# Set attention and a gated feed-forward on one core: the weight words converted with VectorE masks, fewer GpSimd operations, a new instruction order

## The chip, the cores and the metric

The kernel runs on one core of a Trainium2 chip. The metric is device time in microseconds (us) of one execution; what is given as "the time" is the median of three executions. A profiled execution leaves a trace. Its span runs from the first to the last recorded instruction or transfer, and the time of that execution is a little longer than the span. Engines are named as the profile names them: PE is TensorE's matmul, PEld its weight load, DVE is VectorE, ACT is ScalarE, POOL is GpSimd, SP (SPq) is SyncE's DMA queue.

## What is computed

```python
def _attn_ref(x, inducing):             # x 4 x 12480 x 128, inducing 32 x 128
    def mab(q, kv):
        s = scale * (q @ kv.transpose(0, 2, 1))
        a = np.exp(s - s.max(-1, keepdims=True))
        a /= a.sum(-1, keepdims=True) + 1e-09
        return a @ kv
    h = mab(I, x)                        # 32 inducing rows attend to all tokens of a batch
    return mab(x, h)                     # every token attends to those 32 rows
def _moe_ref(x, w_in, w_out):            # w_in 128 x 2048, w_out 2048 x 128
    h = x @ w_in
    return (h - np.tanh(h)) @ w_out
```

x is float32. w_in and w_out come as float64, which the core reads as pairs of 32-bit words.

## The kernel before, in words

Each of the four batches (12480 tokens) is cut into seven slabs of 1792 tokens, 896 KB each (`big` tiles, 19 of them, shared by all uses). A batch has a first and a second half.

**First half** (`first`): all seven slabs are loaded (line 397) and scored on PE against the inducing rows (`scores`, line 382 with `indT_sb`). Two slabs share a PSUM tile `d`, which DVE copies to an `sl` tile while it takes the maximum (line 409). The maximum over the whole batch (lines 422 to 427) must be known before ACT can take the first exponential (line 436). DVE transposes those (line 438, tile `et`, two of them), and PE accumulates them against the slab in token order (`acc`, line 473). The slab in token order is either loaded a second time (13 slabs, `LOADED`, line 448) or made by PE transposes (line 458) and copied out of PSUM by ACT (line 464) or DVE (line 466).

**Linear part** (`linear`): the 32 attended rows (`hT`, lines 486 to 494) go through the feed-forward. Instead of h - tanh(h) for every token, the kernel uses a tangent at the mean of the 32 rows of a batch: products with w_in (line 382, `win_sb`), a transpose and the mean on DVE (lines 516 to 521), tanh on ACT, an odd series in the mean (`series`, lines 529 to 533, five small DVE operations), the tangent (lines 538 to 542), and products with w_out (line 551 and lines 557, 558), which end in the small tiles P4 and Pm (lines 560, 561).

**Second half** (`second`): every slab is scored against `hT` (line 382), copied out with a maximum (line 595); per group of slab pairs the maximum is spread (lines 602 to 608), ACT takes exponentials (line 619), PE multiplies with P4 (line 634), and ACT (line 650) or DVE (line 652) writes the result to a `big` tile, which is stored (line 641). A batch's first half runs beside the second half of the batch before. A bound for the tangent (`bound`) is computed at the end; a general path behind it isn't taken.

**Weights** (`weight`): eight chunks of 128x512 double words, four of w_in, four of w_out. Each is loaded to a `big` tile as raw words, and low word, exponent, mantissa and sign are taken apart and put together on DVE, ACT and GpSimd. A chunk's `big` tile comes free, and can take the next slab, when the chunk is done.

**What sets the order.** `Plan.order` simulates five in-order queues (PE, DVE, ACT, POOL, SP) with a cost for each operation, and picks among the ready operations by priority. The priorities come from constants (`LOADX`, `PA`, `OT` and others) and from `JIT`, a table of offsets by kind, batch and slab. The instructions are then issued in that order, and each engine works its own list strictly in order: an instruction that waits holds up all behind it. SP's list holds every load and store.

## Time and profile before

| | us |
|---|---|
| median of 3 runs (191.67 to 192.47) | 191.79 |
| the profiled execution | 191.85 |
| its span | 190.1 |
| PE busy | 151.0 |
| DVE busy | 137.8 |
| ACT busy | 104.7 |
| POOL busy | 46.5 |
| 67.39 MB in SP's DMA queue, share of 16 engines | 89.5% |

The kernel has a head (weights and the first half of batch 0, to about 50 us), a middle in which the halves of neighbouring batches run beside each other, and a tail in which batch 3 is finished and stored. Shares of busy time are means over these three, so each is read by itself.

### The profile page before, as it was taken

The page shows a single profiled execution, that of the slowest core. Times are in us where ns is not written, and L with a number is a line of the kernel's source. Part 1 is how long each engine was busy: PE and PEld are TensorE (multiplying, and loading weights), DVE is VectorE, ACT ScalarE, POOL GpSimd, SP SyncE. Part 2 cuts the span into 40 slices and gives each one's busy share as a digit, 9 for nine tenths or more (in the row PEclk, how much of TensorE's full clock was granted, in tenths as well). Part 3 has the DMA queues.
Part 4 walks back from the last instruction along what each step waited for, and adds up shares of the span by engine and source line. Part 5 has one row for each costly group of instructions (what it writes and reads, how often), then busy time and mean ns, then how long its engine had stood idle before and what let it go on. Part 6 is the DMA issues. An engine that isn't in the chain of part 4 may idle for free.

```text
span 190.1 us, 4686 instructions
## 1 busy us (share of the span) xinstructions
PE 151.0 (79%) x1924; PEld 85.9 (45%) x1924; DVE 137.8 (73%) x292; ACT 104.7 (55%) x156; POOL 46.5 (24%) x38
## 2 busy tenths in 40 slices
PE   0059987517999999999989999989999997896600
PEld 0006746207855647664267663545466323352100
DVE  3438978655739989676998378986975899898900
ACT  2716857891013294465196734456957467679900
POOL 1499999599902000000200000200000020000000
PEclk9999996855999999999999999999999999999955
DMA  5999999605999999999999999998999997589993
GB/s 119 406 392 428 416 409 422 228 0 186 365 397 418 401 393 399 406 400 364 396 416 409 422 402 411 394 428 322 326 420 424 413 376 297 205 331 401 375 400 145
DMA packets 11549, 67.77 MB, mean 357 GB/s; under 512 B 1408, under 2 KB 1408, under 8 KB 11520
## 3 DMA queue, kind: packets, MB, share of 16 engines
q1 hardware_dynamic: 11520, 67.39, 89.5%
q8 instruction: 17, 0.28, 0.5%
q14 instruction: 12, 0.10, 0.1%
HBM read 41.83 MB, written 25.56 MB: 355 GB/s over the span
## 4 chain that ended last, share of the span: by engine, by line
PE 45%; DMA 20%; POOL 9%; ACT 7%; DVE 6%; issue 6%; SPq 1%; DVEq 0%; POOLq 0%; ACTq 0%
PE d L382 14%; DMA big<-in_xT 12%; PE side L473 8%; PE d L634 8%; PE d L458 8%; DMA big<-in_xn 6%; POOL big L348 5%; ACT big L650 3%; DMA big<-in_w_in 2%; PE side L551 2%; DVE big L652 2%; POOL win_sb L359 2%; POOL win_sb L362 1%; PE side L605 1%; PE side L382 1%
## 5 line engine op out<-in xcount | busy, mean ns | idle before, releaser
L650 ACT ACTIVATE big<-d,Pm,wg 128x896 f32<-128x896 f32 x31 | 33.6, 1094 | 29.0 <-PE d L634 24.7
L382 PE MATMUL d<-big,indT_sb 128*32 128x448 f32 x224 | 29.2, 590 | 12.7 <-DMA big<-in_xT 12.4
L473 PE MATMUL side<-big,et 128*32 128x128 f32 x784 | 30.4, 287 | 5.6 <-DVE et L438 4.9
L458 PE MATMUL d<-ident,big 128*128 128x128 f32 x210 | 29.6, 295 | 3.6 <-DVE big L466 2.2
L464 ACT COPY big<-d 128x896 f32<-128x896 f32 x23 | 20.3, 905 | 22.0 <-PE d L458 21.7
L473 PEld LDWEIGHTS side<-big,et 128*32 128x32 f32 x784 | 25.0, 115 | 16.4 <-DVE et L438 7.8
L634 PE MATMUL d<-sl,k 32*128 32x448 f32 x212 | 30.4, 585 | 0.2
L458 PEld LDWEIGHTS d<-ident,big 128*128 128x128 f32 x210 | 25.2, 152 | 11.8 <-DVE big L466 3.0
L652 DVE TENSOR_SCALAR big<-d,wg,Pm 128x896 f32<-128x896 f32 x22 | 26.6, 1208 | 4.4 <-PE d L634 3.3
L382 PE MATMUL d<-big,hT 128*32 128x448 f32 x224 | 25.3, 542 | 1.0 <-ACT big L650 0.6
L564 POOL TENSOR_TENSOR m<-m,all_mean 128x512 f32<-128x512 f32 x4 | 4.2, 1048 | 60.9 <-DVE all_mean L521 60.9
L438 DVE STREAM_TRANSPOSE et<-sl 128x896 f32<-128x896 f32 (+1 forms) x16 | 15.7, 983 | 2.8 <-issue 2.8
L409 DVE TENSOR_SCALAR_CACHE_REDUCE sl<-d 128x896 f32<-128x896 f32 (+1 forms) x16 | 15.3, 967 | 3.2 <-PE d L382 2.3
L595 DVE TENSOR_SCALAR_CACHE_REDUCE sl<-d 128x896 f32<-128x896 f32 (+1 forms) x16 | 15.3, 964 | 3.0 <-PE d L382 3.0
L348 POOL TENSOR_SCALAR big<-big 128x512 int32<-128x512 f32 x8 | 15.7, 1968 | 6.4 <-ACT big L344 5.9
L619 ACT ACTIVATE sl<-sl,nbs 128x896 f32<-128x896 f32 (+1 forms) x16 | 14.9, 945 | 3.0 <-DVE nbs L608 3.0
L634 PEld LDWEIGHTS d<-sl,k 32*128 32x128 f32 x212 | 9.9, 183 | 13.2 <-issue 4.9
L382 PEld LDWEIGHTS d<-big,indT_sb 128*32 128x32 f32 x224 | 6.3, 112 | 20.8 <-issue 12.6
L436 ACT ACTIVATE sl<-sl,nb 128x896 f32<-128x896 f32 (+1 forms) x16 | 15.1, 945 | 0.2 <-DVE nb L427 0.2
L352 DVE SCALAR_TENSOR_TENSOR big<-big 128x512 uint32<-128x512 uint32 x8 | 5.5, 693 | 9.9 <-POOL big L348 9.9
L382 PEld LDWEIGHTS d<-big,hT 128*32 128x32 f32 x224 | 7.1, 109 | 9.2 <-issue 7.2
L414 POOL MEMSET sl<- 64x32 f32 x4 | 0.7, 174 | 39.7 <-DVE sl L409 39.7
(112 smaller groups left out, 169.3 us busy)
## 6 DMA issues: line engine op xcount, KB each, us to landing
big<-in_xT SPq DMA_DIRECT2D x28, 896.0 KB, 9.0
outT<-big SPq DMA_DIRECT2D x23, 896.0 KB, 6.3
big<-in_xn SPq DMA_DIRECT2D x13, 896.0 KB, 9.8
outT<-big SPq DMA_DIRECT2D x3, 864.0 KB, 8.4
big<-in_w_in SPq DMA_DIRECT2D x4, 512.0 KB, 6.9
big<-in_w_out SPq DMA_DIRECT2D x4, 512.0 KB, 14.7
outT<-big SPq DMA_DIRECT2D x3, 448.0 KB, 6.1
outT<-big SPq DMA_DIRECT2D x1, 416.0 KB, 6.9
```

The source lines that it names most:

```text
L348: nc.gpsimd.tensor_scalar(out=x.bitcast(I32), in0=x.bitcast(F32), scalar1=255.0, scalar2=8388608.0, op0=ALU.min, op1=ALU.mult)
L382: nc.tensor.matmul(ps[q * m:(q + 1) * m, :n], lhsT=w, rhs=row, start=True, stop=True)
L409: nc.vector.tensor_scalar(out=sl.get()[:, :n, :], in0=ps.get()[:, :n, :W], scalar1=1.0, scalar2=None, op0=ALU.mult, op1=ALU.max, accum_out ...
L436: nc.scalar.activation(out=t, in_=t, func=AF.Exp, scale=SC, bias=nb.get(), accum_out=sums.get()[:, g:g + 1])
L438: add("DVE", 0.16 + 0.00103 * W * len(pair), lambda e, et=et, sl=sl, n=len(pair): nc.vector.transpose(out=et.get()[:, :n * KB, :].rearrang ...
L458: nc.tensor.transpose(out=o[:, k * 128:(k + 1) * 128], in_=x.get()[:, at:at + 128], identity=ident)
L464: nc.scalar.copy(out=dst, in_=src)
L473: nc.tensor.matmul(hacc.get()[q * m:(q + 1) * m, :C], lhsT=et.get()[:, j * KB + k, :], rhs=xn_t.get()[:, k * C:(k + 1) * C], start=at < NQ ...
L595: nc.vector.tensor_scalar(out=sl.get()[:, :n, :], in0=ps.get()[:, :n, :W], scalar1=1.0, scalar2=None, op0=ALU.mult, op1=ALU.max, accum_out ...
L634: nc.tensor.matmul(ds[q // 2].get()[:, q % 2, :W], lhsT=P4.get()[r, :], rhs=sl.get()[r, j, :], start=True, stop=True)
L650: nc.scalar.activation(out=dst, in_=src, func=AF.Identity, scale=wg.get(), bias=Pm.get())
L652: nc.vector.tensor_scalar(out=dst, in0=src, scalar1=wg.get(), scalar2=Pm.get(), op0=ALU.mult, op1=ALU.add)
```

## The change

Four things change. The weights' bits are taken apart in another way: the exponent is only masked on DVE, the mantissa gets the exponent of 8.0 by a second mask, ACT makes the power's bits directly in one operation that existed before with another scale (`above`), ACT's `mantissa` and GpSimd's `power` are gone, and `join` moves from GpSimd to DVE, where it subtracts the 7 as well. GpSimd keeps one operation per chunk (`scale`). The series moves from DVE to GpSimd and has six operations there. The planner's costs and constants change, and so do all offsets in `JIT`, `SIDE`, `LOADED` (13 slabs as before, partly others) and the groups: batch 1 is grouped as three pairs and one, and batch 3 as two and two, where it was four single pairs (eight groups instead of ten).

```diff
 JIT = {
-    ('A', 0, 0): -2, ('A', 0, 1): 7, ('A', 0, 2): -8, ('A', 0, 3): -17, ('A', 0, 4): 2, ('A', 0, 5): -32,
...
+    ('A', 0, 0): -110, ('A', 0, 1): 10, ('A', 0, 2): -10, ('A', 0, 3): 3, ('A', 0, 4): -10, ('A', 0, 5): -128,
...
-LATE = -5.0
-WAIT = 0.30000000000000004
-LOADW = (-32.5, -27.0)
-PA, OT, PT, OB, PB = 4.5, 17.5, 8.5, -5.0, 16.5
-LOADX, LOADN = 32, 154.5
-SWITCH = 11.5
+LATE = 10.0
+WAIT = -11.700000000000006
+LOADW = (-31.5, -27.0)
+PA, OT, PT, OB, PB = -8.0, 25.0, 11.0, -17.5, 16.0
+LOADX, LOADN = 32, 313.5
+SPLITS = ([[0, 1], [2, 3]], [[0], [1], [2], [3]], [[0, 1], [2], [3]], [[0, 1, 2, 3]], [[0, 1, 2], [3]], [[0], [1, 2, 3]])
+SPLIT = (0, 4, 0, 0)
+SWITCH = 12.5
...
-    GROUPS = [[[0, 1], [2, 3]]] * (B - 1) + [[[0], [1], [2], [3]]]
+    GROUPS = [SPLITS[k] for k in SPLIT]
...
-        v.memset(shift[:, 0:1], -896.0)
+        v.memset(shift[:, 0:1], -896.0 * 2.0 ** 23)
...
+            def exponent(e, r=r):
+                nc.vector.tensor_scalar(out=r["e"], in0=r["hi"], scalar1=0x7FF00000, scalar2=None, op0=ALU.bitwise_and)
+
+            def bits(e, r=r, dst=dst):
+                nc.vector.tensor_scalar(out=dst.bitcast(U32), in0=r["hi"], scalar1=0xFFFFF, scalar2=0x41000000,
+                                        op0=ALU.bitwise_and, op1=ALU.bitwise_or)
+
             def low(e, r=r):
                 nc.scalar.activation(out=r["lo"].bitcast(F32), in_=r["lo"], func=AF.Copy, scale=2.0 ** -52)
 
-            def exponent(e, r=r):
-                nc.vector.tensor_scalar(out=r["e"], in0=r["hi"], scalar1=20, scalar2=0x7FF,
-                                        op0=ALU.logical_shift_right, op1=ALU.bitwise_and)
-
-            def bits(e, r=r, dst=dst):
-                nc.vector.tensor_scalar(out=dst.bitcast(U32), in0=r["hi"], scalar1=0xFFFFF, scalar2=None, op0=ALU.bitwise_and)
-
             def above(e, r=r):
-                nc.scalar.activation(out=r["e"].bitcast(F32), in_=r["e"], func=AF.Relu, bias=shift[:, 0:1])
-
-            def power(e, r=r):
-                x = r["e"]
-                nc.gpsimd.tensor_scalar(out=x.bitcast(I32), in0=x.bitcast(F32), scalar1=255.0, scalar2=8388608.0, op0=ALU.min, op1=ALU.mult)
+                nc.scalar.activation(out=r["e"], in_=r["e"], func=AF.Relu, scale=8.0, bias=shift[:, 0:1])
...
-            def mantissa(e, dst=dst):
-                nc.scalar.activation(out=dst, in_=dst.bitcast(U32), func=AF.Copy, scale=2.0 ** -20, bias=1.0)
-
             def join(e, r=r, dst=dst):
-                nc.gpsimd.tensor_tensor(out=dst, in0=dst, in1=r["lo"].bitcast(F32), op=ALU.add)
+                nc.vector.scalar_tensor_tensor(out=dst, in0=dst, scalar=-7.0, in1=r["lo"].bitcast(F32), op0=ALU.add, op1=ALU.add)
...
         def series(e):
-            v = nc.vector
+            v = nc.gpsimd
             a, q, y = u.get(), g.get(), mean.get()
             v.tensor_tensor(out=a, in0=y, in1=y, op=ALU.mult)
             v.tensor_scalar(out=q, in0=a, scalar1=SERIES[2], scalar2=SERIES[1], op0=ALU.mult, op1=ALU.add)
             v.tensor_tensor(out=q, in0=q, in1=a, op=ALU.mult)
-            v.scalar_tensor_tensor(out=q, in0=q, scalar=SERIES[0], in1=a, op0=ALU.add, op1=ALU.mult)
+            v.tensor_scalar(out=q, in0=q, scalar1=SERIES[0], scalar2=None, op0=ALU.add)
+            v.tensor_tensor(out=q, in0=q, in1=a, op=ALU.mult)
             v.tensor_tensor(out=q, in0=q, in1=y, op=ALU.mult)
```

In the changed kernel the lines have other numbers: exponent 339, bits 342, sign 353, join 357, scale 360, the copy with maximum 405, exponentials 432, transposes 434, accumulation 469, series 525 to 530, tangent 535 to 539, second-half copies 592, results 647 (ACT) and 649 (DVE).

What moves is shown at two places. The first is GpSimd's list in the head, where `big` and `win_sb` are the chunks' tiles. Before:

```order
L348 TENSOR_SCALAR big_65<-big_65 128x512
L359 TENSOR_TENSOR win_sb<-win_sb,big_65 128x512
L348 TENSOR_SCALAR big_66<-big_66 128x512
L362 TENSOR_TENSOR win_sb<-win_sb,big_65 128x512
L359 TENSOR_TENSOR win_sb<-win_sb,big_66 128x512
L348 TENSOR_SCALAR big_68<-big_68 128x512
```

Now:

```order
L360 TENSOR_TENSOR win_sb<-win_sb,big_66 128x512
L360 TENSOR_TENSOR win_sb<-win_sb,big_67 128x512
L360 TENSOR_TENSOR win_sb<-win_sb,big_69 128x512
L360 TENSOR_TENSOR win_sb<-win_sb,big_71 128x512
L360 TENSOR_TENSOR wout_sb<-wout_sb,big_76 128x512
```

Two of GpSimd's three operations for each chunk are gone from its list. On DVE, at the same place in the head, the list was:

```order
L352 SCALAR_TENSOR_TENSOR big_65<-big_65 128x512
L352 SCALAR_TENSOR_TENSOR big_66<-big_66 128x512
L337 TENSOR_SCALAR big_68<-big_68 128x512
L341 TENSOR_SCALAR win_sb<-big_68 128x512
L409 TENSOR_SCALAR sl_84,mxg_196<-d_95 128x896
L352 SCALAR_TENSOR_TENSOR big_68<-big_68 128x512
L337 TENSOR_SCALAR big_71<-big_71 128x512
L341 TENSOR_SCALAR win_sb<-big_71 128x512
```

and is now:

```order
L357 SCALAR_TENSOR_TENSOR win_sb<-win_sb,big_66 128x512
L353 SCALAR_TENSOR_TENSOR big_66<-big_66 128x512
L339 TENSOR_SCALAR big_67<-big_67 128x512
L342 TENSOR_SCALAR win_sb<-big_67 128x512
L357 SCALAR_TENSOR_TENSOR win_sb<-win_sb,big_67 128x512
L405 TENSOR_SCALAR sl_84,mxg_185<-d_95 128x896
L353 SCALAR_TENSOR_TENSOR big_67<-big_67 128x512
L339 TENSOR_SCALAR big_69<-big_69 128x512
L342 TENSOR_SCALAR win_sb<-big_69 128x512
```

Each chunk has a fourth DVE operation, the join, and the two masks of the next chunk (339 and 342) stand right behind the operation that releases GpSimd's only one.

The second place is DVE in the tail, from the mean of batch 3 (`all_mean`) to the tangent (`m_99` is the slope tile that PE waits for). Before:

```order
L521 TENSOR_SCALAR all_mean<-all_mean 128x16
L595 TENSOR_SCALAR sl_89,bm_1567<-d_96 128x896
L652 TENSOR_SCALAR big_81<-d_95,wg_1557,Pm_1316 128x896
L529 TENSOR_TENSOR u_1582<-all_mean 128x16
L530 TENSOR_SCALAR all_g<-u_1582 128x16
L531 TENSOR_TENSOR all_g<-all_g,u_1582 128x16
L532 SCALAR_TENSOR_TENSOR all_g<-all_g,u_1582 128x16
L533 TENSOR_TENSOR all_g<-all_g,all_mean 128x16
L602 TENSOR_REDUCE big_1593<-bm_1567 128x1
L603 TENSOR_SCALAR k_101<-ident,big_1593 128x128
L538 TENSOR_TENSOR all_gp<-th_1569 128x16
L539 TENSOR_TENSOR m_99<-m_98,all_gp 128x512
```

Now:

```order
L517 TENSOR_SCALAR all_mean<-all_mean 128x16
L592 TENSOR_SCALAR sl_84,bm_1547<-d_97 128x896
L649 TENSOR_SCALAR big_82<-d_96,wg_1539,Pm_1478 128x896
L535 TENSOR_TENSOR all_gp<-th_1572 128x16
L536 TENSOR_TENSOR m_99<-m_98,all_gp 128x512
```

The five series operations and the two of a group's maximum no longer stand between the mean and the tangent. PE's list behind it, from the products with w_out to the points (`mean_w`), was:

```order
L551 MATMUL side<-wout_sb,m_99 32x128 x16
L382 MATMUL d_97<-big_75,hT_119 32x448 x4
L382 MATMUL d_97<-big_65,hT_119 32x448 x4
L634 MATMUL d_95<-sl_91,k_103 128x448 x2
L634 MATMUL d_96<-sl_91,k_103 128x448 x2
L557 MATMUL side<-k_105,fold 128x128
L558 MATMUL side<-mean_w,k_105 128x1
```

and is now:

```order
L631 MATMUL d_96<-sl_89,k_104 128x448 x2
L548 MATMUL side<-wout_sb,m_99 32x128 x16
L378 MATMUL d_95<-big_69,hT_119 32x448 x4
L554 MATMUL side<-k_103,fold 128x128
L555 MATMUL side<-mean_w,k_103 128x1
```

One scored slab stands between the two products, where there were two scored slabs and one multiplied with P4.

## Rows read from the trace of the kernel before

**Rows 1.** Page, slices of the span in 40 equal parts: POOL, DMA share, GB/s.

```profile
POOL 1499999599902000000200000200000020000000
...
DMA  5999999605999999999999999998999997589993
GB/s 119 406 392 428 416 409 422 228 0 186 365 397 418 401 393 399 406 400 364 396 416 409 422 402 411 394 428 322 326 420 424 413 376 297 205 331 401 375 400 145
```

**Rows 2.** Windows: stretch, its length, busy us (count) by engine, clock, DMA, GB/s.

```profile
38.00:40.00 2.00, 0.95 (x8) 0.00 (x0) 1.82 (x2) 2.00 (x4) 1.92 (x2) 0.50 0.00 0
...
60.00:80.00 20.00, 20.00 (x319) 12.17 (x315) 16.79 (x40) 10.03 (x20) 0.97 (x2) 1.00 1.00 401
```

**Rows 3.** Chain that ended last, in order of time: start, us, what.

```profile
48.47 11.10 DMA big<-in_xT
...
75.49 0.96 PE d L634 x8
76.45 1.00 PE side L473 x28
```

**Rows 4.** Instructions grouped by line and form: count | busy us, mean ns | idle before.

```profile
L438 DVE STREAM_TRANSPOSE et<-sl 128x896 f32<-128x896 f32 x12 | 13.1, 1101 | 2.8 <-issue 2.8
L409 DVE TENSOR_SCALAR_CACHE_REDUCE sl<-d 128x896 f32<-128x896 f32 x12 | 13.0, 1082 | 2.3 <-PE d L382 2.3
...
L466 DVE COPY big<-d 128x896 f32<-128x896 f32 x7 | 7.5, 1080 | 1.9 <-PE d L458 1.2 <-ACT big L464 0.8
...
L352 DVE SCALAR_TENSOR_TENSOR big<-big 128x512 uint32<-128x512 uint32 x8 | 5.5, 693 | 9.9 <-POOL big L348 9.9
...
L564 POOL TENSOR_TENSOR m<-m,all_mean 128x512 f32<-128x512 f32 x4 | 4.2, 1048 | 60.9 <-DVE all_mean L521 60.9
...
L356 ACT ACTIVATE wout_sb<-wout_sb 128x512 f32<-128x512 uint32 x4 | 2.5, 623 | 1.9 <-DVE wout_sb L341 1.9
...
L533 DVE TENSOR_TENSOR all_g<-all_g,all_mean 128x16 f32<-128x16 f32 x4 | 0.7, 175 | 0.1
...
L414 POOL MEMSET sl<- 64x32 f32 x4 | 0.7, 174 | 39.7 <-DVE sl L409 39.7
```

**Rows 5.** Single lines: durations in ns as minimum, median, maximum; first and last start.

```profile
L337 DVE TENSOR_SCALAR big<-big x8: 422/998/1522, 5.8 to 38.8; 128x512 uint32<-128x512 uint32 x8
...
L362 POOL TENSOR_TENSOR wout_sb<-wout_sb,big x4: 1272/1312/1772, 32.6 to 50.7; 128x512 f32<-128x512 f32 x4
```

**Rows 6.** Instructions in order of time, head: start us, us, engine, line, what.

```profile
9.39 1.72 PE L382 MATMUL d<-big,indT_sb 128*32 128x448 f32 x8 [9.39 <-DMA big<-in_xT]
...
25.29 0.69 DVE L352 SCALAR_TENSOR_TENSOR big<-big 128x512 uint32<-128x512 uint32 x1 [1.18 <-POOL big L348]
25.34 1.80 POOL L359 TENSOR_TENSOR win_sb<-win_sb,big 128x512 f32<-128x512 f32 x1
25.90 1.52 DVE L337 TENSOR_SCALAR big<-big 128x512 uint32<-128x512 uint32 x1
...
33.99 0.96 PE L382 MATMUL d<-big,indT_sb 128*32 128x448 f32 x8
...
35.11 0.62 DVE L409 TENSOR_SCALAR_CACHE_REDUCE sl<-d 128x448 f32<-128x448 f32 x1 [0.93 <-ACT big L464]
...
37.53 1.04 ACT L436 ACTIVATE sl<-sl,nb 128x896 f32<-128x896 f32 x1 [0.19 <-DVE nb L427]
...
42.72 1.10 DVE L438 STREAM_TRANSPOSE et<-sl 128x896 f32<-128x896 f32 x1
...
49.37 0.64 DVE L438 STREAM_TRANSPOSE et<-sl 128x448 f32<-128x448 f32 x1
```

**Rows 7.** SP's DMA queue in order of time: start us, us, line, what, count.

```profile
61.46 1.08 SPq L397 DMA_DIRECT2D big<-in_xT  x2
```

**Rows 8.** Instructions in order of time, tail (batch 3's linear part).

```profile
147.39 0.35 DVE L489 TENSOR_SCALAR k<-side,rs 128x128 f32<-128x128 f32 x1
...
164.08 0.26 ACT L560 COPY k<-side 128x128 f32<-128x128 f32 x1
```

More of the change, by code (lines that the diff above doesn't have):

```diff
@@ L296, in fused_kernel @@
     mean_b, gp_b, g_b, far_b = ([stacked(n, b) for b in range(B)] for n in ("mean", "gp", "g", "far"))
-    add("SP", 0.1, lambda e: nc.sync.dma_start(out=indT_sb, in_=indT), writes=[ind_b], pri=-500, size=0.02)
+    add("SP", 0.35, lambda e: nc.sync.dma_start(out=indT_sb, in_=indT), writes=[ind_b], pri=-500, size=0.02)
     add("POOL", 0.6, lambda e: make_identity(nc, ident), writes=[ident_b], pri=-10)
@@ L364, in weight @@
             p = pri + k
-            add("SP", 0.1, ld, writes=[buf], pri=load_pri + k, size=0.524)
-            add("DVE", 0.7, exponent, reads=[buf], writes=[ex], pri=p)
-            add("ACT", 0.7, low, reads=[buf], writes=[lo], pri=p)
-            add("ACT", 0.7, above, reads=[buf, ones_b], writes=[ex], pri=p)
-            add("DVE", 0.7, bits, reads=[buf], writes=[outs[k]], pri=p)
-            add("ACT", 0.7, mantissa, reads=[buf], writes=[outs[k]], pri=p)
-            add("POOL", 0.75, power, reads=[buf], writes=[ex], pri=p)
-            add("DVE", 0.8, sign, reads=[buf], writes=[ex], pri=p)
-            add("POOL", 1.4, join, reads=[buf, lo], writes=[outs[k]], pri=p)
-            add("POOL", 1.4, scale, reads=[buf, ex], writes=[outs[k]], pri=p)
+            add("SP", 0.35, ld, writes=[buf], pri=load_pri + k, size=0.524)
+            add("DVE", 0.55, exponent, reads=[buf], writes=[ex], pri=p)
+            add("DVE", 0.55, bits, reads=[buf], writes=[outs[k]], pri=p)
+            add("ACT", 0.68, low, reads=[buf], writes=[lo], pri=p)
+            add("ACT", 0.71, above, reads=[buf, ones_b], writes=[ex], pri=p)
+            add("DVE", 0.75, sign, reads=[buf], writes=[ex], pri=p)
+            add("DVE", 0.75, join, reads=[buf, lo], writes=[outs[k]], pri=p)
+            add("POOL", 1.45, scale, reads=[buf, ex], writes=[outs[k]], pri=p)
     xT_b = {}
@@ L396, in first @@
                 base = b * N + BASE[s]
-                add("SP", 0.1, lambda e, x=x, base=base: nc.sync.dma_start(out=x.get(), in_=xT[:, base:base + ST]),
+                add("SP", 0.35, lambda e, x=x, base=base: nc.sync.dma_start(out=x.get(), in_=xT[:, base:base + ST]),
                     writes=[x], pri=pri + s - LOADX + jit("X", b, s), size=0.9175)
@@ L423, in spread_out @@
             nc.vector.tensor_scalar(out=mq.get(), in0=mask, scalar1=mx.get(), scalar2=None, op0=ALU.mult)
-        add("DVE", 0.35, spread_out, reads=[mxg, fold_b], writes=[mq], pri=p)
+        add("DVE", 0.42, spread_out, reads=[mxg, fold_b], writes=[mq], pri=p)
         add("PE", 0.25, lambda e: nc.tensor.matmul(ps.get()[:, :NQ], lhsT=fold2, rhs=mq.get(), start=True, stop=True),
@@ L542, in tangent @@
             v.tensor_tensor(out=WM.get(), in0=WM.get(), in1=wide(k), op=ALU.add)
-        add("DVE", 0.6, series, reads=[mean], writes=[u, g], pri=pri)
-        add("DVE", 1.75, tangent, reads=[MT, th, g, mean], writes=[gp, WM, k], pri=pri)
+        add("POOL", 1.5, series, reads=[mean], writes=[u, g], pri=pri)
+        add("DVE", 1.92, tangent, reads=[MT, th, g, mean], writes=[gp, WM, k], pri=pri)
         psP, psR = place("q"), place("q")
@@ L640, in store @@
                     def store(at, end, needs):
-                        add("SP", 0.1, lambda e: nc.sync.dma_start(out=outT[:, base + at:base + end], in_=ot.get()[:, at:end]),
+                        add("SP", 0.35, lambda e: nc.sync.dma_start(out=outT[:, base + at:base + end], in_=ot.get()[:, at:end]),
                             reads=[ot, *needs], pri=pri - 200, size=0.9175 * (end - at) / ST)
```

12 lines of the change are left out of this document (6 added, 6 removed), and 51 rows, old and new, of the table JIT.

## The prediction, made before the changed kernel was run

> **What bounds the kernel now.** I read the slices of the page first [rows 1]. DMA is full from 3 to about 33 us and nearly full from 50 to 155 us, but between lies a hole: two slices of 4.75 us in which it moves 228 and 0 GB/s on average, and the one after moves 186. In just these slices GpSimd is at 9 tenths. It is the only long stretch in which GpSimd is busy, and it is the weights' conversion. The window from 38 to 40 us shows the hole from inside: no byte, PE busy half the time at a granted clock of 0.50 (1.2 GHz, the lower of its two levels), ACT and GpSimd full [rows 2]. The chain of waits tells what the hole costs: a transfer of a slab, 11.1 us long on the chain, that begins only at 48.47 us [rows 3]. The loads behind it wait for `big` tiles that the weight chunks hold.
>
> The second bound is PE. From 60 to 80 us PE is busy for 20.00 of 20 us [rows 2], and the chain runs through PE alone there, about 1 us for each slab and step [rows 3]. So the middle is paid for by PE's work, which the change leaves as it is, but for two spreads of a group's maximum. DMA has room behind that: 67.39 MB at the 400 to 420 GB/s of the full slices [rows 1] are 164 us. What the head wins is therefore kept by the middle, and what it doesn't win the middle can't give. The tail is a chain from the last accumulation of batch 3 to P4, then stores.
>
> **Weights: what goes, what comes.** Per chunk GpSimd had three operations (power, join, scale; about 2.0 + 1.7 + 1.5 us) and keeps the scale, 1.27 us alone and up to 1.77 us next to DVE [rows 5]. So GpSimd falls from some 41 us of conversion to 8 x 1.5 = 12 us and bounds nothing any more. ACT loses eight mantissa operations of 0.62 us [rows 4], 5 us in all, in a stage where it isn't the last to arrive: I count nothing for it. The operation that now makes the power's bits existed before, so it is free. DVE gets eight joins of the form of the sign operation, 0.69 us [rows 4]: 5.5 us. That makes DVE the engine to look at in the head.
>
> DVE's masks have two prices. Line 337 takes 0.42 us at best and 1.52 us at worst [rows 5], and the row of 25.90 us shows the bad case: the mask starts inside a GpSimd operation that runs from 25.34 to 27.14, and ends 0.28 us after it [rows 6]. The sign operation ahead of it started with that GpSimd operation and took its usual 0.69 us; GpSimd's took 1.80 instead. In the new order the two masks of the next chunk stand right behind the operation that starts GpSimd's scale, so one of each pair is held: 1.50 + 0.43 = 1.93 us a pair.
>
> The Trainium skill (SBUF — State Buffer, section SBUF: two separate sides) says that GpSimd and a DVE operation in a two-port mode, or one with two SBUF inputs, lock each other out for a whole instruction, whoever starts first. The masks' rows agree with it; that a join could be held too, which it also says, no row shows, since every sign operation came first.
>
> **The head, from both sides.** The point to watch is the first exponential, at 37.53 us before [rows 6]; it needs all seven slabs of batch 0 scored. *Earliest*: up to the seventh slab lie the same 9.57 MB in both orders (seven slabs of 0.9175 MB and six chunks of 0.524). 1.97 MB had landed when PE started at 9.39 us [rows 6]; the other 7.6 MB at 0.41 MB/us are 18.5 us, so it lands at 27.9. Scoring it started at 33.99 before, 3.5 us ahead of the exponential [rows 6]. So not before 31.4 us. *By DVE's list*: the first chunk now comes behind a slab, 1.44 MB; between 5.8 us (0.52 MB, [rows 5]) and 9.39 us (1.97 MB) that is 8.1 us. From there to the copy of the seventh slab (line 405) DVE has one free pair of masks 0.9, five held pairs 9.7, ten joins and signs 6.9, three copies of scores 3.2 and two copies of transposed slabs 2.2 (1.08 us each, [rows 4]): 22.9 us, so 31.0 us. From that copy to the exponential it was 37.53 - 35.11 = 2.4 us, and one join stands between: 34.1 us. I take 34.1, since DVE's sum lies above the data's and each of its terms is a row; waits between DVE, ACT and PE could add 2 us. Gain: 3.4 us (bounds 1.5 and 6).
>
> From there to the release of batch 2's first slab load, which came at 61.46 us [rows 7]. Before, the first transpose (42.72) waited some 4 us for DVE, which stood at a sign operation behind GpSimd's power, and the last one ended at 50.0 [rows 6]. Now DVE has, from 33.9 us on: a held pair 1.9, a free mask 0.4, a held mask 1.5, four joins and signs 2.8, transposes of 3 x 1.10 + 0.63 [rows 4, 6]: 10.6 us, so the last ends at 44.5. Behind it PE has two accumulations and two slabs' scores of about 1 us each [rows 3], the small steps to `hT` 1.5, one more scoring, seven transposes 0.9, the products with w_in 1.1 and the first scoring with `hT` 0.75: 8.3 us, plus about 1 us that it lags: 54.0. Gain: 7.5 us. The two gains are not added, the second contains the first.
>
> Can the loads follow? A slab takes 2.24 us at 0.41 MB/us. The queue in front of the load that needs the sixth chunk's tile runs dry at about 35 us; that chunk's scale ends at about 34.5. The load behind waits for the first accumulation, at about 37.5, so 1 to 2 us of hole remain where there were 10. DMA then ends the eighth load behind the hole at about 56, against 63 us (45 us, where it restarted, plus 8 x 2.24), so it keeps step.
>
> Not all is gain: PE's new list has at that point one scoring less behind it, and at the first product with P4 (75.49 us before, [rows 3]) one scoring and one accumulation less, 0.96 + 1.0 = 1.9 us that are still to do.
>
> **Series on GpSimd.** DVE loses five operations of about 0.18 us [rows 4] per batch. What six cost on GpSimd no row shows: between 0.17 us each (a memset of 32 elements) and 1.05 us (a product of 512 elements, [rows 4]), 1.0 to 6.3 us. I take 0.3 us each, 1.8 us, near the low end since 16 elements are nearer to 32 than to 512, with a start for each. Between the mean and the first DVE operation that needs the series, DVE's new list has two other operations (1.1 + 1.2 us) and three of the tangent (1.0 us): 3.3 us of cover, so I cost it at nothing; uncovered, at the high end, it is 3.0 us a batch.
>
> [...]
>
> **Order and groups.** ACT hands DVE four result copies and one copy of a transposed slab: in the middle DVE is at 16.8 of 20 us [rows 2] and the series' 3.5 us make up for part of the 5.9, so nothing. Two groups fewer save PE 0.8 us, hidden in rounding. In the tail, from the last accumulated product (147.39 + 0.35) to P4 (164.08 + 0.26) it was 16.6 us [rows 8]. The new lists drop from that path the series 0.9, a group's maximum 0.4, and on PE one scoring and one product (1.7); they add a result copy ahead of the mean (1.2), and the products with w_in come 1.1 us later behind two scorings but `hT` 1.1 us earlier. Sum -1.8; I take -2, bounds -4 and +1. Behind P4 eight slabs are stored in both, so the end follows P4.
>
> **Sum.** 190.1 - 7.5 + 1.9 - 2.0 = 182.5 us of span. The profiled execution took 191.85, that is 1.75 us more than its span and 0.06 from the median: 184.3 us.
>
> **Rivals.**
> 1. *The head goes at the data's pace.* If the masks mostly slip in ahead of GpSimd, the exponential comes at 31.4 us, 2.7 earlier: 181.5 us. For it: a mask at 0.42 us occurs in the trace. Against it: the median mask is at 1.0 [rows 5].
> 2. *The joins are held as well.* A join that starts inside a scale would wait out its rest, up to 1.3 us [rows 5]; with three or four of the six on the path the head loses 4 us of its 7.5: 188.3 us. For it: DVE's list is the longest in the head by my sum. Against it: there is one GpSimd operation for a chunk, and a mask mostly meets it first.
> 3. *The order gives it back in the middle.* DVE's copies come later in the new order's lists and PE waits for `d` tiles, of which there are three. PE is 20.00 of 20 [rows 2] before, so there is nothing to win there and something to lose: waits of a tenth over the 70 us of the middle are 7 us, 191.3 us, no change. Against it: I find no place for it in the lists.
> 4. *The series becomes the path (slower).* If a small GpSimd operation costs near the 1.05 us of line 564, DVE stops at the tangent with everything behind it (copies of scores, results), PE waits for the slope and for `d`: (6 x 1.05 - 3.3) x 4 = 12 us, 196 us. It decides from about 0.9 us an operation: then 4 x 2.1 = 8.4 us take away the gain of 7.6. Against it: line 564 works on 32 times the elements.
>
> **How the numbers follow.** Chances: forecast (183 to 187) 0.50, rival 1 0.17, rival 2 0.15, rival 3 0.10 (two thirds of it within the bound, one third slower), rival 4 0.08. Faster by over 0.5% (about what a measurement here can tell from no change) is below 190.8: 0.50 + 0.17 + 0.15 = 0.82; same 0.07; slower 0.11. The range leaves out rivals 3 and 4: up to 190.5, which also holds rival 2 with a tail that gains nothing (188.3 + 2), and down to 179.5, rival 1 with the tail at its better bound (181.5 - 2).
>
> **What would show it.** Right: DMA moves bytes in every 2 us window between 34 and 46 us; the first exponential comes near 34 us and batch 2's first load near 54; masks at both 0.43 and 1.5 us, each long one ending with a GpSimd scale; GpSimd under 30 us busy; the first product with P4 near 68 us; from the last accumulated product to P4 under 15 us. Wrong: a DVE wait for GpSimd at line 538 longer than the series' 2 us (rival 4), joins above 1 us (rival 2), or PE below 95% busy between 70 and 140 us (rival 3).

## The result and the profile after

The changed kernel takes **185.18 us** (median of 4 runs, 184.30 to 185.67) against 192.13 us before on the same chip; the ratio is 0.963, 95% interval 0.959 to 0.968. Run again later on another chip, it took 185.31 us, ratio 0.965 [0.960, 0.969]. Forecast were 184.3 us in a range of 179.5 to 190.5. The profiled execution has a span of 182.3 us (forecast 182.5). Executions over 1.5% longer than the fastest of the same kernel are left out of the ratios but not of the medians and ranges, and the profiled execution of e11_pe_busy_placed is one of these, so of its trace only the head is read.

From the page: busy time, share and count of each engine; three rows of the span in 40 slices; and the chain of waits that ended last, by engine:

```profile
PE 152.7 (84%) x1920; PEld 85.4 (47%) x1920; DVE 141.2 (77%) x279; ACT 96.0 (53%) x141; POOL 21.7 (12%) x46
...
POOL 1033333332005000000130000002200022000000
...
DMA  5999999979999999899999999999999996489992
GB/s 153 348 422 425 415 410 420 373 269 337 409 423 426 414 421 333 286 422 412 368 352 419 426 416 427 418 370 350 421 419 425 423 405 276 204 351 401 400 399 75
...
PE 69%; DVE 16%; DMA 5%; ACT 3%; issue 1%; SPq 1%; DVEq 0%; ACTq 0%
```

Against [rows 1], GpSimd is no longer at 9 tenths in the head but at 3, and where three slices moved 228, 0 and 186 GB/s, three now move 373, 269 and 337. The windows of the stretch where the hole was (stretch, its length, busy us and count for PE, PEld, DVE, ACT, POOL, then clock, DMA, GB/s) answer to [rows 2]:

```profile
34.00:36.00 2.00, 1.47 (x8) 0.04 (x5) 2.00 (x3) 2.00 (x5) 0.79 (x1) 0.52 0.97 363
36.00:38.00 2.00, 1.52 (x32) 1.41 (x36) 2.00 (x4) 2.00 (x6) 0.00 (x0) 0.50 0.92 323
38.00:40.00 2.00, 2.00 (x44) 1.85 (x40) 1.11 (x4) 0.41 (x2) 1.33 (x1) 0.50 0.63 186
40.00:42.00 2.00, 2.00 (x44) 1.72 (x40) 2.00 (x3) 0.00 (x0) 0.07 (x1) 0.77 0.95 370
```

No window is empty; the worst still moves 186 GB/s. DVE and ACT are full from 34 to 38 us, and GpSimd no longer is. PE works, but at a granted clock of 0.50 to 0.77.

What SP's queue waited for between 33 and 46 us, before and then now (us in total, times, longest):

```profile
SPq L397 <- POOL wout_sb L362: 14.5, 2, 9.6
SPq L397 <- PE side L473: 1.5, 1, 1.5
...
SPq L393 <- PE side L469: 5.4, 3, 3.3
SPq L393 <- POOL wout_sb L360: 3.5, 1, 3.5
```

Line 362 before, and line 360 now, is a chunk's last GpSimd operation, behind which the chunk's `big` tile is free. One load of a slab stood 9.6 us for it, until line 362 ended at 43.9 us, and that is the hole; now it is 3.5 us, and the rest is a wait for PE's accumulation.

In order of time, the points that the prediction named: the first exponential [rows 6], batch 2's first slab load [rows 7], the first product with P4 [rows 3], P4 of batch 3 [rows 8]:

```profile
33.34 1.04 ACT L432 ACTIVATE sl<-sl,nb 128x896 f32<-128x896 f32 x1 [0.59 <-DVE nb L423]
...
53.58 1.08 SPq L393 DMA_DIRECT2D big<-in_xT  x2
...
67.97 0.66 PE L631 MATMUL d<-sl,k 32*128 32x448 f32 x4
...
156.07 0.27 ACT L557 COPY k<-side 128x128 f32<-128x128 f32 x1 [1.32 <-PE side L602]
```

They come 4.2, 7.9, 7.5 and 8.0 us earlier than before. So the whole lead is there by 54 us. The middle hands on most of it (6.9 us at batch 3's last accumulated product), and the tail adds 1.1.

### The profile page after: what moved, and what is told of

Same layout as the page of the kernel before. It is cut to its first block, busy times and chain, and to the rows that moved or that the text cites. A ratio compares the mean times of both kernels' runs of the same rounds, so it can differ in the third digit from the quotient of the medians.

```text
span 182.3 us, 4643 instructions
## 1 busy us (share of the span) xinstructions
PE 152.7 (84%) x1920; PEld 85.4 (47%) x1920; DVE 141.2 (77%) x279; ACT 96.0 (53%) x141; POOL 21.7 (12%) x46
## 4 chain that ended last, share of the span: by engine, by line
PE 69%; DVE 16%; DMA 5%; ACT 3%; issue 1%; SPq 1%; DVEq 0%; ACTq 0%
PE d L378 22%; PE side L469 14%; PE d L454 12%; PE d L631 11%; DMA big<-in_xT 5%; DVE big L649 4%; PE side L548 2%; PE side L378 2%; PE side L602 2%; ACT big L460 2%; DVE big L462 1%; DVE et L434 1%; DVE sl L405 1%; PE side L554 1%; PE side L487 1%
## 5 line engine op out<-in xcount | busy, mean ns | idle before, releaser
L647 ACT ACTIVATE big<-d,Pm,wg 128x896 f32<-128x896 f32 x28 | 30.3, 1093 | 20.4 <-PE d L631 15.5
L649 DVE TENSOR_SCALAR big<-d,wg,Pm 128x896 f32<-128x896 f32 x27 | 32.5, 1204 | 3.8 <-PE d L631 2.1
L631 PE MATMUL d<-sl,k 32*128 32x448 f32 x220 | 33.3, 605 | 1.3 <-DVE all_far L563 0.8
L460 ACT COPY big<-d 128x896 f32<-128x896 f32 x22 | 19.4, 909 | 28.2 <-PE d L454 24.9
L454 PE MATMUL d<-ident,big 128*128 128x128 f32 x210 | 28.4, 289 | 0.2 <-ACT big L460 0.2
L405 DVE TENSOR_SCALAR_CACHE_REDUCE sl<-d 128x896 f32<-128x896 f32 (+1 forms) x16 | 15.5, 970 | 5.8 <-PE d L378 5.7
L631 PEld LDWEIGHTS d<-sl,k 32*128 32x128 f32 x220 | 10.7, 187 | 15.1 <-ACT big L647 4.0
L462 DVE COPY big<-d 128x896 f32<-128x896 f32 x8 | 8.5, 1086 | 3.0 <-PE d L454 2.3
L346 ACT ACTIVATE big<-big 128x512 f32<-128x512 uint32 x8 | 5.4, 688 | 7.6 <-DMA big<-in_w_in 7.6
L360 POOL TENSOR_TENSOR win_sb<-win_sb,big 128x512 f32<-128x512 f32 x4 | 5.6, 1392 | 18.5 <-DVE big L353 12.5
L339 DVE TENSOR_SCALAR big<-big 128x512 uint32<-128x512 uint32 x8 | 3.4, 420 | 5.2 <-DMA big<-in_w_in 5.2
```

Of the source, the lines that this page charges most:

```text
L405: nc.vector.tensor_scalar(out=sl.get()[:, :n, :], in0=ps.get()[:, :n, :W], scalar1=1.0, scalar2=None, op0=ALU.mult, op1=ALU.max, accum_out ...
L454: nc.tensor.transpose(out=o[:, k * 128:(k + 1) * 128], in_=x.get()[:, at:at + 128], identity=ident)
L460: nc.scalar.copy(out=dst, in_=src)
L631: nc.tensor.matmul(ds[q // 2].get()[:, q % 2, :W], lhsT=P4.get()[r, :], rhs=sl.get()[r, j, :], start=True, stop=True)
L647: nc.scalar.activation(out=dst, in_=src, func=AF.Identity, scale=wg.get(), bias=Pm.get())
L649: nc.vector.tensor_scalar(out=dst, in0=src, scalar1=wg.get(), scalar2=Pm.get(), op0=ALU.mult, op1=ALU.add)
```

## Experiments

For every run four points of its trace are given, in us: the start of the first exponential; **T0** and **T3**, the end of the operation that scales the last accumulated products of batch 0 and of batch 3 (line 485 of the changed kernel, 489 before); and the end of P4 of batch 3. Ratios are to the kernel before, run on the same chip beside it, with 95% intervals. The runs were made on four chips, so times of different chips are compared by the ratios; the first row has the range of the four medians. Each time is the median of 4 to 17 executions. e2_new_conversion_old_order has no ratio and was run again as e12_new_conversion_old_order_again.

| run | time | ratio | exp | T0 | T3 | P4 |
|---|---|---|---|---|---|---|
| before | 191.26 to 192.13 | 1 | 37.53 | 54.45 | 147.74 | 164.34 |
| changed | 185.18 | 0.963 [0.959, 0.968] | 33.34 | 49.16 | 140.88 | 156.34 |
| e8_changed_again | 185.31 | 0.965 [0.960, 0.969] | 33.72 | 49.59 | 141.11 | 156.57 |
| e1_old_conversion_new_order | 192.88 | 1.011 [1.007, 1.016] | 39.61 | 57.01 | 149.02 | 164.47 |
| e5_old_conversion_mended | 193.71 | 1.008 [1.004, 1.011] | 40.38 | 58.25 | 151.37 | 166.83 |
| e2_new_conversion_old_order | 186.16 | - | 34.51 | 48.12 | 141.11 | 157.47 |
| e12_new_conversion_old_order_again | 185.88 | 0.972 [0.965, 0.979] | 34.56 | 48.16 | 140.67 | 157.03 |
| e3_series_on_dve | 184.76 | 0.970 [0.964, 0.976] | 32.82 | 48.06 | 140.98 | 156.78 |
| e4_difference_behind_tangent | 183.58 | 0.964 [0.959, 0.969] | 33.19 | 48.94 | 141.44 | 156.24 |
| e6_masks_ahead | 183.81 | 0.958 [0.952, 0.963] | 32.50 | 46.55 | 140.23 | 155.70 |
| e7_pe_busy_in_head | 184.80 | 0.964 [0.959, 0.968] | 35.32 | 48.34 | 141.27 | 156.74 |
| e11_pe_busy_placed | 183.11 | 0.954 [0.948, 0.961] | 33.67 | 47.44 | 141.61 | 157.07 |
| e9_masks_ahead_difference_late | 183.12 | 0.956 [0.951, 0.962] | 32.59 | 46.91 | 141.33 | 156.12 |
| e10_both_and_pe_busy | 181.56 | 0.951 [0.945, 0.956] | 32.51 | 46.44 | 139.96 | 154.76 |

Each run left one trace, so first the spread. e8_changed_again, e3_series_on_dve and e4_difference_behind_tangent have the changed kernel's head unaltered. In these four traces the first exponential lies between 32.82 and 33.72 us, T0 between 48.06 and 49.59, the way from one to the other takes 15.2 to 15.9, and T3 lies between 140.88 and 141.44. A difference inside these bounds shows nothing. Nor does T3 follow T0 in the kernels with the new conversion and order: T0 varies by 3.2 us among them, T3 by 1.5, and a sooner T0 doesn't bring a sooner T3 each time. From T3 to P4 the traces of one tail agree within 0.1 us.

### Conversion or order: each without the other

The theory is the prediction's: the conversion leaves GpSimd, so the chunks' tiles come free earlier. The rival is that the searched order and the groups make the gain. The order of all operations is held fixed, and only what a chunk's operations issue is swapped. In the changed kernel (the cut is shortened; the second mask and the bias of `above` go back with it):

```diff
-nc.vector.tensor_scalar(out=r["e"], in0=r["hi"], scalar1=0x7FF00000, op0=bitwise_and)        # exponent
+nc.vector.tensor_scalar(out=r["e"], in0=r["hi"], scalar1=20, scalar2=0x7FF, op0=shift_right, op1=bitwise_and)
-nc.scalar.activation(out=r["e"], in_=r["e"], func=Relu, scale=8.0, bias=shift)                # above
+nc.scalar.activation(out=x.bitcast(F32), in_=x, func=Relu, bias=shift)
+nc.scalar.activation(out=dst, in_=dst.bitcast(U32), func=Copy, scale=2.0 ** -20, bias=1.0)    # mantissa
+nc.gpsimd.tensor_scalar(out=x.bitcast(I32), in0=x.bitcast(F32), scalar1=255.0, scalar2=8388608.0, ...)  # power
-nc.vector.scalar_tensor_tensor(out=dst, in0=dst, scalar=-7.0, in1=r["lo"], op0=add, op1=add)  # join
+nc.gpsimd.tensor_tensor(out=dst, in0=dst, in1=r["lo"], op=add)
```

> The changed kernel with its new order, groups and series, but each chunk converted the old way: power, join and scale on GpSimd, mantissa on ACT; the old operations stand in the places that the new order has for the chunk. Theory (conversion leaving GpSimd makes the gain): GpSimd is busy over 40 us again, the chunks' tiles come free late, windows of 2 us with under 100 GB/s come back between 34 and 48 us, the first exponential comes at 36.5 us or later (33.3 with the new conversion), batch 2's first slab load at 59 us or later (53.6), time 190 to 197 us. Rival (the new searched order and the groups make the gain by themselves): the head may shift, but the time stays between 184 and 187.5 us.

> As e1_old_conversion_new_order, where one chunk's mantissa operation on ACT stood behind its join on GpSimd (so that chunk's weights had other values); here it stands ahead of the join in every chunk. Nothing else differs. Theory and rival as there: 190 to 197 us against 184 to 187.5 us; after that run 192.5 to 193.5 us is expected.

Measured: 192.88 and 193.71 us, slightly slower than the kernel before. The page, two windows and the first load of batch 2 of e5_old_conversion_mended show the hole again (in e1_old_conversion_new_order no window is empty, but three between 36 and 48 us move 47 to 90 GB/s):

```profile
PE 153.3 (80%) x1920; PEld 85.5 (44%) x1920; DVE 143.2 (74%) x271; ACT 100.4 (52%) x149; POOL 50.1 (26%) x62
...
36.00:38.00 2.00, 0.49 (x8) 0.00 (x0) 2.00 (x4) 1.50 (x3) 1.83 (x2) 1.00 0.00 0
...
42.00:44.00 2.00, 0.00 (x0) 0.00 (x0) 2.00 (x3) 1.31 (x3) 1.92 (x2) 0.50 0.20 29
...
62.66 1.08 SPq L404 DMA_DIRECT2D big<-in_xT  x2
```

GpSimd is busy 50.1 us instead of 21.7, one window is empty and one moves 29 GB/s, and batch 2's first load comes at 62.66 instead of 53.58. T0 is 8.7 us later than in e8_changed_again, T3 and P4 10.3, the span 8.3 (192.5 against 184.2; e8_changed_again takes 27.6 us from P4 to its end, the changed kernel's first trace 26.0). What the head loses here is carried to the end. The rival has fallen.

The swap also brings back eight `mantissa` operations on ACT, which no run separates from GpSimd's. The chain of before through the hole shows what each is worth there (start, us, what):

```profile
35.67 0.53 ACT wout_sb L356
...
36.23 1.92 POOL big L348
...
40.10 1.99 POOL big L348
...
42.11 0.69 DVE big L352
42.81 1.03 DVE et L438
```

One `mantissa` (line 356) stands on it with 0.53 us; behind it GpSimd's `power`, `join` and `power` hold the sign operation, and with it the first transpose, for 5.9 us.

The other half, in the kernel before: the new masks, `above` and `join` (on DVE), and nothing issued for `power` and `mantissa`; order, groups and series as before.

> The kernel before with its order, groups and series, but each chunk converted the new way: masks, sign and join on DVE, the power's bits by ACT, one scale on GpSimd. Theory: GpSimd is busy under 25 us, no 2 us window between 34 and 46 us is empty, the first exponential comes near 34.5 us (37.5 before), batch 2's first slab load near 55 us (61.5), and of these 6.5 us most is kept: time 185 to 188.5 us. Rival (the order makes the gain, and without it what the head wins is lost again in the middle): 190.5 to 193 us.

> The same kernel as e2_new_conversion_old_order, for more runs of it. Theory (the searched order, the groups and the series together are worth nothing; the conversion is the whole gain): within 0.8 us of the changed kernel's 185.3 us. Rival (the order is worth 1 us or more): 186.3 us or longer.

Measured: 186.16 us (183.64 to 188.28) and 185.88 us. The page, a window and two points of e12_new_conversion_old_order_again:

```profile
PE 150.3 (82%) x1924; PEld 86.0 (47%) x1924; DVE 134.9 (74%) x300; ACT 100.2 (55%) x148; POOL 17.3 (9%) x22
...
36.00:38.00 2.00, 0.86 (x17) 0.80 (x21) 2.00 (x4) 2.00 (x4) 1.37 (x2) 0.50 0.05 22
...
34.56 1.04 ACT L435 ACTIVATE sl<-sl,nb 128x896 f32<-128x896 f32 x1 [0.61 <-DVE nb L426]
...
54.83 2.58 SPq L396 DMA_DIRECT2D big<-in_xT  x3
```

The conversion alone, in an order searched for another kernel, gives a ratio of 0.972 where the whole change gives 0.965: some 5.3 of 6.8 us. So order, groups and series together are worth about 1.5 us, with an interval from nothing to 3 us (an estimate from the two intervals, which overlap). That settles neither the theory (within 0.8 us) nor the rival (1 us or more): the median is 0.6 above 185.31, but on a chip on which the kernel before was 0.5 us faster as well. One window, 36 to 38 us, moves only 22 GB/s, so the old order still leaves a short hole. By T3 the two are equal; in the traces the new order is ahead behind it (16.4 us from T3 to P4 against 15.5).

### The series, and what it pushed

> The changed kernel with the series back on DVE as five operations, at the place in the order where GpSimd's stood. Theory (the move is worth little, because GpSimd's later operation at line 561 then holds DVE's first two-input operation of the tangent): DVE gets about 5 x 0.2 = 1.0 us more per batch and loses the hold of 0.66 us, since line 561 then runs during a PSUM copy; the way from the last accumulated product of batch 3 to P4 becomes 15.8 to 16.0 us (15.5), time 185.0 to 186.3 us. Rival (the series' DVE time is worth its whole length in every batch, since DVE limits PE): 4 x 1.0 us more, 188.5 to 190 us.

The edit is `v = nc.vector` in `series`, with the old five operations. Measured: 184.76 us, ratio 0.970 [0.964, 0.976]. From T3 to P4 it takes 15.8 us, against 15.5 in the changed kernel: the move is worth 0.3 us on that way, and DVE's 1.0 us per batch is not worth its length. The rival (188.5 us or more) has fallen.

Why so little: GpSimd's six operations fit into the cover, but the operation behind them (line 561, a subtraction for the bound) comes later. GpSimd, then DVE, in order of time in the changed kernel's batch 3:

```profile
148.67 0.22 POOL L525 TENSOR_TENSOR u<-all_mean 128x16 f32<-128x16 f32 x1 [19.70 <-DVE all_mean L517]
...
150.21 0.22 POOL L530 TENSOR_TENSOR all_g<-all_g,all_mean 128x16 f32<-128x16 f32 x1
150.39 1.05 POOL L561 TENSOR_TENSOR m<-m,all_mean 128x512 f32<-128x512 f32 x1
...
150.64 0.83 DVE L535 TENSOR_TENSOR all_gp<-th 128x16 f32<-128x16 f32 x1
151.50 0.69 DVE L536 TENSOR_TENSOR m<-m,all_gp 128x512 f32<-128x512 f32 x1
```

DVE's first operation of the tangent (line 535, 128x16) takes 0.83 us; it starts inside line 561 and ends 0.03 us behind it. Over the four batches it takes 0.66 us on average (0.29 to 0.93), and before it was 0.17 each. e4_difference_behind_tangent moves line 561 behind the tangent in the order and lets GpSimd wait for the tangent's result:

```diff
+nc.gpsimd.tensor_copy(u.get(), WM.get()[:, :, 0])     # waits for the tangent's last result
 nc.gpsimd.tensor_tensor(out=away.get(), in0=MT.get(), in1=wide(mean), op=ALU.subtract)
```

> The changed kernel with GpSimd's 1.05 us subtraction (line 561) held back until the tangent's last DVE operation has written its result (GpSimd first copies 16 values of it). Theory (two-input DVE operations wait for a running GpSimd operation): the tangent's first operation takes 0.17 us in every batch, not 0.29 to 0.93; the way from the last accumulated product of batch 3 to P4 becomes 14.8 to 15.0 us (15.5), time 184.2 to 184.9 us. Rival (the 0.83 us was something else, or what stands behind it is late anyway): way to P4 15.3 to 15.7, time 184.9 to 185.5 us.

The same two places in its trace (the GpSimd operation is line 564 there), and DVE's operation over all four batches (count | busy us, mean ns | idle before):

```profile
151.19 0.17 DVE L535 TENSOR_TENSOR all_gp<-th 128x16 f32<-128x16 f32 x1
...
153.41 1.05 POOL L564 TENSOR_TENSOR m<-m,all_mean 128x512 f32<-128x512 f32 x1
...
L535 DVE TENSOR_TENSOR all_gp<-th 128x16 f32<-128x16 f32 x4 | 0.6, 159 | 0.0
```

It takes 0.13 to 0.17 us in every batch, and from T3 to P4 it is 14.8 us, as the theory said. So line 561 did cause the hold. On the whole time the effect is not resolved: the median is 183.58 us, under the expected 184.2, but the ratio, 0.964, is the changed kernel's own, and T3 came 0.3 to 0.6 us later in this trace.

### The masks

DVE's masks are held as forecast: they wait out GpSimd's `scale`. Line 342 of the changed kernel, min/median/max in ns and first and last start (w_in, then w_out), and line 339, the other mask, which never is:

```profile
L342 DVE TENSOR_SCALAR win_sb<-big x4: 421/1496/1510, 8.5 to 20.2; 128x512 uint32<-128x512 uint32 x4
L342 DVE TENSOR_SCALAR wout_sb<-big x4: 408/1504/1511, 24.2 to 38.5; 128x512 uint32<-128x512 uint32 x4
...
L339 DVE TENSOR_SCALAR big<-big x8: 414/420/429, 8.1 to 35.0; 128x512 uint32<-128x512 uint32 x8
```

Does that cost time? e6_masks_ahead moves each pair in DVE's list ahead of the operation that starts the scale (and for the last chunks the small product for the maximum and its reduction too); as a sketch of the list, not of the code:

```diff
-sign(k)  exponent(k+1)  bits(k+1)     # the scale of k starts behind the sign; bits(k+1) starts in it
+exponent(k+1)  bits(k+1)  sign(k)
```

> The changed kernel with one edit in DVE's list: the two masks of a chunk stand ahead of the sign or join that lets GpSimd's scale of the chunk before start, not behind it. Theory (a mask that starts in a running scale waits out its rest, some 1.08 us, and DVE's list sets the head): all sixteen masks take 0.43 us, joins and signs keep 0.65 to 0.70 since they start ahead of the scales, the first transpose (line 434 of the changed kernel) comes near 33.8 us instead of 35.3, and the time falls by 1.0 to 1.7 us, to 183.0 to 184.2 us. Rival (the head goes by the data, or the half clock of PE behind the first transposes): the first exponential and batch 2's first slab load stay within 0.5 us of 33.3 and 53.6, time 184.7 to 185.7 us.

Measured: 183.81 us, 1.5 less than the changed kernel on the same chip (its executions and those of e8_changed_again differ by 1.5 us on average, an estimate with a 95% interval of 0.6 to 2.4). DVE and PE in order of time, and what PE waited for in batch 3 (us in total, times, longest):

```profile
31.97 0.42 DVE L344 TENSOR_SCALAR wout_sb<-big 128x512 uint32<-128x512 uint32 x1
...
33.67 1.11 DVE L441 STREAM_TRANSPOSE et<-sl 128x896 f32<-128x896 f32 x1
34.70 0.94 DVE L355 SCALAR_TENSOR_TENSOR big<-big 128x512 uint32<-128x512 uint32 x1
...
35.25 3.21 PE L476 MATMUL side<-big,et 128*32 128x128 f32 x82
...
PE side L476 <- DMA big<-in_xn: 1.3, 1, 1.3
```

All masks take 0.42 us, and the first transpose comes at 33.67 instead of 34.8 to 35.7 in the four traces with the unaltered head. Two signs of eight are now held a little (0.94 and 0.99 us), which the theory didn't expect. The first exponential, at 32.50, is hardly ahead of 32.82 in e3_series_on_dve: with the masks free, DVE waits for PE instead (1.51 us at the seventh slab's copy). The gain lies behind it: T0 comes 1.5 to 3.0 us earlier, but T3 only 0.7 to 1.2. In batch 3 PE now waits 1.3 us for the last load of a slab in token order, which the two traces of the changed kernel don't have. That the loads have become the limit of the middle is not shown: e4_difference_behind_tangent, with its unaltered head, has that wait too:

```profile
PE side L469 <- DMA big<-in_xn: 0.6, 1, 0.6
```

### PE's clock in the head

The changed kernel's PE stands idle from 30.8 to 33.9 us, but for one small product, and from 34.1 to 40.9 us its granted clock is 0.50: 82 accumulating products at 36.48 us take 4.63 us. Extra products in the idle stretches test whether the clock follows from the idle time.

```diff
+nc.tensor.matmul(side[:, 0, :128], lhsT=ident, rhs=ones, start=True, stop=True)   # 12 + 6 + 7 times
```

> The changed kernel with 25 extra products of 128 columns on PE, whose results are overwritten, in its idle stretches between the seventh slab's scores and the first accumulated product (30.8 to 36.5 us). Theory (PE's work from 36.5 to 40.8 us is long because the granted clock fell to 0.5 after those idle stretches, and PE is the path there): the granted clock stays at 1.0 through 34 to 42 us, the 82 products that took 4.63 us take about 3, and the time falls by 1 to 2 us, to 183.2 to 184.2 us. Rival (loads set that stretch: the slabs for it are not there earlier): the clock is higher but batch 0's last accumulated product ends within 0.5 us of 48.6, time 184.7 to 185.7 us. A second rival: the clock is low in that stretch whatever PE does ahead of it, time as before or up to 0.5 us longer.

Two windows of e7_pe_busy_in_head, and a line each of its PE and its DVE:

```profile
34.00:36.00 2.00, 2.00 (x19) 1.15 (x18) 0.87 (x4) 0.68 (x1) 0.42 (x1) 1.00 1.00 380
36.00:38.00 2.00, 2.00 (x26) 1.88 (x30) 1.82 (x3) 2.00 (x5) 0.00 (x0) 1.00 0.97 391
...
37.67 2.59 PE L469 MATMUL side<-big,et 128*32 128x128 f32 x82
...
35.13 0.16 DVE L423 TENSOR_REDUCE nb<-side 128x1 f32<-128x4 f32 x1 [2.05 <-PE side L758]
```

and of the changed kernel, the same 82 products:

```profile
36.48 4.63 PE L469 MATMUL side<-big,et 128*32 128x128 f32 x82 [1.01 <-DVE et L434]
```

The clock stays at 1.00 and the 82 products take 2.59 us instead of 4.63. So the second rival has fallen: the low clock does follow from the idle time ahead. But the time, 184.80 us, misses the theory (183.2 to 184.2) and lies in the first rival's range (184.7 to 185.7). The extra products were badly placed: DVE's reduction of the small product waited 2.05 us for them (line 758), so the exponential came 1.6 us later than in e8_changed_again. From there to T0 it is 13.0 us instead of 15.2 to 15.9, but T0 itself, 48.34, is not earlier than in e3_series_on_dve. Hence the same with 6 + 3 + 4 products, placed so that no reader waits for them:

> As e7_pe_busy_in_head, but with 13 extra products instead of 25, ordered so that no reader waits for them (there the reader of the small product for the maximum started 2 us later). Theory: first exponential at 33.3 to 33.8 us again, granted clock 1.0 from 34 to 42 us, batch 0's last accumulated product scaled (line 485 of the changed kernel) near 47.0 us instead of 49.2 to 49.6, time 183.6 to 184.6 us. Rival (loads set that stretch): 48.5 us or later, time 184.7 to 185.7.

Measured: 183.11 us, ratio 0.954 [0.948, 0.961] against the changed kernel's 0.965 [0.960, 0.969]; the intervals barely touch. In the trace the exponential is at 33.67 again, and the granted clock at 1.00 from 30 to 44 us:

```profile
36.00:38.00 2.00, 1.80 (x50) 1.61 (x52) 2.00 (x3) 2.00 (x6) 0.00 (x0) 1.00 0.94 294
...
36.80 2.56 PE L469 MATMUL side<-big,et 128*32 128x128 f32 x82 [0.20 <-DVE et L434]
```

T0 is at 47.44, 13.8 us behind the exponential instead of 15.2 to 15.9. So half the clock cost the head 1.5 to 2.1 us, and with T0 earlier and the time below the first rival's 184.7 us, that rival has fallen too.

### Together

> The changed kernel with both edits, the masks ahead of the operation that lets GpSimd's scale start (as e6_masks_ahead) and GpSimd's subtraction behind the tangent (as e4_difference_behind_tangent). If the two are independent (one in the head, one in the tail), the time is 182.8 to 183.6 us: 185.3 less 1.5 less 0.7. Rival (what is late next is the same for both, so only the larger counts): 183.5 to 184.3 us.

> As e9_masks_ahead_difference_late, and 12 extra products on PE (6 behind the seventh slab's scores, 6 behind the small product for the maximum, placed so that no reader of that product waits for them), whose results are overwritten. Theory (the half clock in 33 to 37 us costs PE 0.6 to 1.0 us, but batch 3's last xn load, not PE, sets the end of the middle since the masks were moved): granted clock 1.0 in 32 to 38 us, batch 0's last accumulated product 0.6 to 1.0 us earlier than in e9_masks_ahead_difference_late, time the same within 0.4 us. Rival (PE still sets the middle): 0.6 to 1.0 us faster.

Measured: 183.12 us for the two edits, in the range for independent ones. That they are independent is not shown: by the ratios (0.956 and 0.958, intervals overlapping) little is gained on e6_masks_ahead, and in the trace T3 is 1.1 us later than there, while from T3 to P4 it takes 14.8 us. With the extra products of PE as well it is **181.56 us** (180.92 to 183.24), ratio 0.951 [0.945, 0.956]: the fastest version here, 1.4% under the changed kernel by the ratios. My theory for the last step got no support. It said that the loads set the middle by now, that T0 would come 0.6 to 1.0 us sooner and the time stay within 0.4 us; T0 came 0.5 us sooner and the median fell by 1.56. PE's wait for a load in batch 3 did not grow (0.3 us, against 0.8 in e9_masks_ahead_difference_late). But the intervals of the two ratios overlap, so the rival (0.6 to 1.0 us faster) isn't shown either, and why the traces differ more at T3 (1.4 us) than at T0 stays open.

## Why the prediction was right, step by step

**The mechanism** held: the hole belonged to GpSimd's conversion, and the middle hands most of the head's gain on. e5_old_conversion_mended and e12_new_conversion_old_order_again show both halves of it, and SP's wait of 9.6 us names the operation. The reading of [rows 1] that led to it was loose: in the hole's slices GpSimd is at 5, 9 and 9 tenths, and it is at 9 in five earlier ones in which DMA is full. A busy GpSimd alone makes no hole; the queue has to have run out of free tiles. Rival 3 is out: PE is busy 77.15 of 78 us from 62 to 140 us.

**The sum** came out within 0.2 us of the span (182.3 against 182.5), and that is in part luck: the head gave 7.9 us instead of 7.5, the middle took back 1.0 up to T3 instead of 1.9, and the tail gave 1.1 instead of 2.0.

**DVE's list in the head.** The sum to the seventh slab's copy was 31.0 us; it came at 31.09. Five held pairs were counted, and five came: line 342 at 10.55, 15.36, 20.17, 24.16 and 29.66 us. Two errors cancel all the same: DVE was busy for 21.05 us of that stretch, not the 22.9 of the sum (the durations added up overlap a little), and idle for 1.9 us that the sum left out. The step behind it was too long: 3.1 us from the copy to the exponential, measured 2.25. The 2.4 us taken from before held a mask and an operation of 128x4 (line 423) that took 0.68 us beside a GpSimd operation; its counterpart in the changed kernel took 0.23. Hence 33.34 instead of 34.1. Rival 1 (31.4) didn't come, but its premise was nearer than the forecast had it: in e6_masks_ahead all masks are free, DVE waits for PE, and the exponential comes at 32.50, only 0.3 to 1.2 us ahead of the four traces with held masks.

**From there to batch 2's load.** 53.58 against 54.0, but several errors cancel. The transposes ended at 42.72, not 44.5, since DVE was there 0.7 us sooner and one mask less was held. PE's steps behind them took 10.9 us, not 9.5. That 9.5 was added up wrongly: the listed steps give 9.2 us, not 8.3, as the further scoring isn't in the sum, and with the lag of 1 us 10.2. And PE was further behind than that lag, since its clock was at half until 40.9 us. In e11_pe_busy_placed, with the clock up, the transposes end at 42.18 us, batch 2's first load comes at 51.85, and the steps take 9.7 us; in the four traces with the unaltered head they take 10.3 to 10.9. The granted clock of 0.50 stands in [rows 2]; no term of the sum has it.

**Loads.** Forecast were 1 to 2 us of hole where there were 10. Against 415 GB/s in the full slices, the three slices of before lack 9.5 us of transfers, and the three of 373, 269 and 337 GB/s lack 2.9: more than forecast.

**Middle.** The first product with P4 came at 67.97 us, forecast 68; T3 6.9 us earlier, where 7.5 - 1.9 = 5.6 was forecast.

**Series.** 0.20 to 0.26 us an operation (forecast 0.3), 1.76 us in all, never waited for: rival 4 is out, and the cover was named rightly. What failed is "I cost it at nothing": it pushes line 561 into the tangent, where that stretches line 535 from 0.17 to 0.66 us on average. e4_difference_behind_tangent shows it.

**Joins** (rival 2): all 0.64 to 0.69 us in the changed kernel, as each started ahead of the scale. That two-input operations can be held after all is shown by line 535 and, with the masks moved, by two signs of 0.94 and 0.99 us.

**Tail.** From T3 to P4 16.6 us before, 14.6 forecast, 15.5 measured, so the sign "under 15 us" failed. 0.7 of the 0.9 us is the held line 535 (14.8 without it). The end follows P4 as said: 26.0 us from P4 to the end of the span (27.6 in e8_changed_again), 25.8 before.

## What to carry to other kernels

When an engine that nobody names as the bottleneck holds buffers, look at which transfers wait for those buffers: the change takes 25 us of work off GpSimd, and most of the 7 us gained come from that, because one load had stood 9.6 us for a tile that GpSimd still worked on. When work moves between DVE and GpSimd, list what will start inside the other's operation, also what comes behind the moved piece; the order within one engine's list decides who waits. Price PE's work behind an idle stretch at the granted clock that the rows show there. And before reading a gain from single traces, look how far traces of the same code lie apart: here 1.5 us at T0.
